# Carrying a running phase between token groups by a one-row transfer instead of running sums and half of the carry products

## The chip, the cores and the metric

The kernel runs on one core of a Trainium2 chip. The metric is device time in microseconds (us); results below are medians of executions. Each execution also has a mean granted TensorE clock (1.0 is full speed). With a single core, "slow" only labels an execution over 1.5% above the fastest of the same kernel in the same call.

A word on names: PE is TensorE, DVE VectorE, ACT ScalarE, POOL GpSimd. "L302" is line 302 of that kernel's source; the changed kernel is 12 lines shorter, so the same line has a smaller number there.

## The reference

The work is a gated linear attention with complex decay, followed by a gated mixture feed-forward block. What matters here is the phase.

```python
batch, n_heads, seq, head_dim = (4, 8, 768, 48)
a_re_n, a_im_n = (a_re * scale, a_im * scale)      # scale limits |a| to 0.999
for t in range(S):
    new_re = ar * S_re - ai * S_im                 # state times a complex number
    new_im = ar * S_im + ai * S_re
    S_re, S_im = (new_re + k_t v_t^T, new_im)
    y[t] = q_t . S_re
# ... then, on x = y of 3072 tokens x 384:
g = x @ w_gate                                     # 384 x 1536
ffn_out = (gelu(g) * (x @ w_val)) @ w_out
out = x + sigmoid(x @ w_res) * ffn_out
```

(Condensed.) A product of complex numbers over tokens is a product of magnitudes and a sum of angles. So the kernel needs, for every head and channel (8 x 48 = 384 columns), the running sum of angles over 768 tokens of a batch.

## The kernel before

The 3072 tokens are cut into 12 groups of 256 tokens: four batches times three groups (s = 0, 1, 2), the batches taken in turn. A group lies on 128 partitions in two halves (c = 0, 1). Groups are worked in units: [0], [1,2], [3,4] ... [11]. While one unit is in its attention and output phase, the angles of the next unit are summed. A sum over tokens is a sum over partitions, so it is a TensorE product with a triangular matrix. What earlier groups and halves leave behind comes in as a second product, with a matrix of equal elements (`ones2pi`), over a tile that holds the running sum of the batch's earlier angle tiles (from the second half of its first group on).

```python
    def carry(g):
        b, s = ORD[g]
        if s > 0:
            P = T["R", b]
            nc.vector.tensor_tensor(out=P, in0=P, in1=T["th", g][:, 0:DM], op=OP.add)      # L279
            T["P", g] = P

    def carry_on(g):
        b, s = ORD[g]
        if s == 0:
            T["R", b] = st1.tile([128, DM], FP, tag="R%d" % b, name="R")
            nc.vector.tensor_copy(out=T["R", b], in_=T["th", g][:, DM:W])                  # L287
        elif s < NS - 1:
            nc.vector.tensor_tensor(out=T["R", b], in0=T["R", b], in1=T["th", g][:, DM:W], op=OP.add)   # L289

    def cs_t(g, c):
        # ... (tiles named, cut)
        cs = psM.tile([128, DM], FP, tag="mm", padded_shape=[128, 512], name="cst")
        nc.tensor.matmul(out=cs, lhsT=tmat[c], rhs=th[:, sl], start=True, stop=(s == 0))   # L300
        if s > 0:
            nc.tensor.matmul(out=cs, lhsT=ones2pi, rhs=T["P", g], start=False, stop=True)  # L302
        f = T["f", g]                                                                      # phase in turns,
        nc.vector.tensor_scalar(out=f[:, sl], in0=cs, scalar1=MAGIC, scalar2=MAGIC, op0=OP.add, op1=OP.subtract)
        nc.vector.tensor_tensor(out=f[:, sl], in0=cs, in1=f[:, sl], op=OP.subtract)        # less whole turns
        if c == C - 1:
            carry_on(g)
            # ... (absolute value for the cosine, cut)
```

`tmat[1]` is a triangular matrix that sums the tokens up to each token; `tmat[0]` is the same matrix less its constant. The trick lies in the difference: with P holding half 0 of this group, the product with `ones2pi` adds the whole of half 0, which the negative triangle of `tmat[0]` then corrects. One tile P so serves both halves.

The place of these steps in the program is set by a list of steps that is woven with the others by fractions of the stage:

```python
        cst = [f for g in g1 for f in [call(carry, g)] + [call(cs_t, g, c) for c in range(C)]]
        # ...
            weave((0.0, 0.05, pn[:2]), (0.06, 0.1, csls), (0.12, 0.25, pn[2:]), (0.26, 0.4, exs),
                  # ... (cut)
                  (0.5, 0.5, dec), (0.55, 0.65, atn), (0.62, 0.8, cst), (0.9, 0.95, sin), ...)
            return
        # ...
        weave((0.0, 0.12, csls), ..., (0.46, 0.46, dec), (0.2, 0.65, cst), (0.7, 0.95, atn + sin), ...)
```

Of the kernel before, what the change touches and what calls it, by code (L numbers as in the profile page):

```python
# [9 lines left out]
FP = mybir.dt.float32  # L10
BF = mybir.dt.bfloat16
AF = mybir.ActivationFunctionType
OP = mybir.AluOpType
# [3 lines left out]
def weave(*streams):  # L17

    order = []
    for si, (begin, end, steps) in enumerate(streams):  # L20
        n = len(steps)
        for i, step in enumerate(steps):
            order.append((begin + (end - begin) * (i + 0.5) / n, si, i, step))
    for _, _, _, step in sorted(order, key=lambda e: e[:3]):
        step()
# [3 lines left out]
def kernel(  # L29
# [13 lines left out]
    nc = tc.nc  # L43
    B, H, S, D = q.shape
    DD = 2 * D
    DM = H * D
# [3 lines left out]
    C = 2  # L50
    W = C * DM
    NS = S // (128 * C)
# [3 lines left out]
    ORD = [(b, s) for s in range(NS) for b in range(B)]  # L56
# [19 lines left out]
    tmat = []  # L76
# [9 lines left out]
    ones2pi = singles.tile([128, 128], FP, name="ones2pi")  # L86
# [28 lines left out]
    st1 = ctx.enter_context(tc.tile_pool(name="st1", bufs=1))  # L115
# [13 lines left out]
    T = {}  # L129
# [78 lines left out]
    def squares(g):  # L208

        def q0():  # L210
            T["lm", g] = pS.tile([128, W], FP, tag="s", name="lm")
            with paced("gelu"):
                nc.scalar.activation(out=T["lm", g], in_=flat(T["ar", g]), func=AF.Square)

        def q1():
            if g < 5:
                if g == 0:
                    T["sq"] = hb.tile([128, 4, 2, DM], FP, tag="h2", name="sq0")
                t = T["sq"][:, g % 4].rearrange("p a m -> p (a m)")
            else:  # L220
                t = pE.tile([128, W], FP, tag="E", name="sq")
            T["sq", g] = t
            if g in DVSQ:
                nc.vector.tensor_tensor(out=t, in0=flat(T["ai", g]), in1=flat(T["ai", g]), op=OP.mult)
            else:
                with paced("gelu"):
                    nc.scalar.activation(out=t, in_=flat(T["ai", g]), func=AF.Square)  # L227

        def q2():
            with paced("gmul"):  # L230
                nc.vector.tensor_tensor(out=T["lm", g], in0=T["lm", g], in1=T["sq", g], op=OP.add)  # L231
        return [q0, q1, q2]

    def p1_steps(g):

        def s0():
            lm = T["lm", g]
            act(out=lm, in_=lm, func=AF.Ln)
            nc.vector.tensor_scalar(out=lm, in0=lm, scalar1=0.5, scalar2=LNMAX, op0=OP.mult, op1=OP.min)  # L239

        def s1():
            ar = flat(T["ar", g])
            T["s", g] = pE.tile([128, W], FP, tag="E" if g == 1 else "Ei", name="ra") if g in (1, 2) else ar
            act(out=T["s", g], in_=ar, func=AF.Ln)

        def s2():
            T["th", g] = flat(T["ai", g])
            act(out=T["s", g], in_=T["s", g], func=AF.Exp, scale=-1.0)
            nc.vector.tensor_tensor(out=T["th", g], in0=T["s", g], in1=T["th", g], op=OP.mult)
        return [s0, s1, s2]  # L250
# [5 lines left out]
    def cs_l(g, c):  # L256
        if c == 0:
            if g == 0:
                t = hb.tile([128, 4, DM], FP, tag="sg", name="E0")
                T["E", g] = t[:, 0:2].rearrange("p a m -> p (a m)")  # L260
                T["Ei", g] = t[:, 2:4].rearrange("p a m -> p (a m)")
            else:
                T["E", g] = pE.tile([128, W], FP, tag="E", name="E")
                T["Ei", g] = pE.tile([128, W], FP, tag="Ei", name="Ei")
        sl = slice(c * DM, (c + 1) * DM)
        cs = psM.tile([128, DM], FP, tag="mm", padded_shape=[128, 512], name="csl")
        nc.tensor.matmul(out=cs, lhsT=lmat[c], rhs=T["lm", g][:, sl], start=True, stop=True)  # L267

        def ex():
            act(out=T["E", g][:, sl], in_=cs, func=AF.Exp)  # L270
            act(out=T["Ei", g][:, sl], in_=cs, func=AF.Exp, scale=-1.0)
        return ex

    def carry(g):

        b, s = ORD[g]
        if s > 0:
            P = T["R", b]
            nc.vector.tensor_tensor(out=P, in0=P, in1=T["th", g][:, 0:DM], op=OP.add)  # L279
            T["P", g] = P  # L280

    def carry_on(g):

        b, s = ORD[g]
        if s == 0:
            T["R", b] = st1.tile([128, DM], FP, tag="R%d" % b, name="R")
            nc.vector.tensor_copy(out=T["R", b], in_=T["th", g][:, DM:W])  # L287
        elif s < NS - 1:
            nc.vector.tensor_tensor(out=T["R", b], in0=T["R", b], in1=T["th", g][:, DM:W], op=OP.add)  # L289

    def cs_t(g, c):
        s = ORD[g][1]
        th = T["th", g]
        if c == 0:
            if ("f", g) not in T:
                T["f", g] = T["lm", g]
            T["af", g] = th
        sl = slice(c * DM, (c + 1) * DM)
        cs = psM.tile([128, DM], FP, tag="mm", padded_shape=[128, 512], name="cst")
        nc.tensor.matmul(out=cs, lhsT=tmat[c], rhs=th[:, sl], start=True, stop=(s == 0))  # L300
        if s > 0:
            nc.tensor.matmul(out=cs, lhsT=ones2pi, rhs=T["P", g], start=False, stop=True)  # L302
        f = T["f", g]
        nc.vector.tensor_scalar(out=f[:, sl], in0=cs, scalar1=MAGIC, scalar2=MAGIC, op0=OP.add, op1=OP.subtract)
        nc.vector.tensor_tensor(out=f[:, sl], in0=cs, in1=f[:, sl], op=OP.subtract)
        if c == C - 1:
            carry_on(g)
            T["abs"] = nc.vector.tensor_scalar(out=T["af", g].bitcast(mybir.dt.int32), in0=f.bitcast(mybir.dt.int32),
                                    scalar1=0x7FFFFFFF, scalar2=None, op0=OP.bitwise_and)

# [317 lines left out]
    def gs(u):  # L628
        return UNITS[u] if 0 <= u < NU else []
# [7 lines left out]
    def call(f, *a):  # L637
        return lambda: f(*a)
# [4 lines left out]
    def att_steps(u, half):  # L643

        todo = [(g, c, i * C + c) for i, g in enumerate(gs(u)) for c in range(C)]
        n = len(todo) // 2
        steps = []
        for i, (g, c, jj) in enumerate(todo[half * n:half * n + n]):
            steps += attention(g, c)
            if i > 0:  # L650
                steps.insert(-1, call(xt_step, u, jj - 1))
        if n:
            steps.append(call(xt_step, u, half * n + n - 1))
        return steps

    def phase_x(u):

        pend = []
        g1 = gs(u + 1)
        p1g = [g for w in range(NU) if P1AT.get(w, w - 2) == u for g in gs(w)]  # L660
        now = [g for g in p1g if g in g1]
        ahead = [g for g in p1g if g not in g1]
        ops = [call(op_step, u - 1, jj) for jj in range(len(gs(u - 1)) * C)]
        att = att_steps(u, 1)
        if not g1:
            weave((0.0, 0.8, att), (0.1, 1.0, ops))
            return

        def csl(g, c):
            pend.append(cs_l(g, c))  # L670

        def ex():
            pend.pop(0)()

        def p1(g):
            return (squares(g) if g == HELD else []) + p1_steps(g) + [call(decay0, g)]
        csls = [call(csl, g, c) for g in g1 for c in range(C)]
        exs = [ex for _ in g1 for _ in range(C)]
        dec = [call(decay2, g) for g in g1]
        cst = [f for g in g1 for f in [call(carry, g)] + [call(cs_t, g, c) for c in range(C)]]  # L680
        sin = [call(p2_sin, g) for g in g1]
        table("natural_log_exp_and_others")()
        if now:
            atn = [table("trig_and_small")] + [call(p1_arctan, g) for g in now + ahead]
            pn = zip_steps([p1(g) for g in now])
            weave((0.0, 0.05, pn[:2]), (0.06, 0.1, csls), (0.12, 0.25, pn[2:]), (0.26, 0.4, exs),
                  (0.28, 0.48, zip_steps([p1(g) for g in ahead])),
                  (0.5, 0.5, dec), (0.55, 0.65, atn), (0.62, 0.8, cst), (0.9, 0.95, sin),
                  (0.0, 0.8, att), (0.0, 0.25, ops) if u == 1 else (0.1, 1.0, ops))
            return  # L690
        atn = [table("trig_and_small")] + [call(p1_arctan, g) for g in ahead]
        weave((0.0, 0.12, csls), (0.05, 0.5, zip_steps([p1(g) for g in ahead])), (0.12, 0.45, exs),
              (0.46, 0.46, dec), (0.2, 0.65, cst), (0.7, 0.95, atn + sin), (0.0, 0.8, att), (0.1, 1.0, ops))
# [141 lines left out]
```

## Time and profile before

The median was 298.79 us (298.38 to 299.6) over three executions. The profiled execution has a span of 297.3 us.

From 119 us on, the kernel is a string of alternating stages, and three and a half of them hold the angle sums. The windows view of the kernel before (columns: from and to, length, then busy us and records of each engine, clock, DMA share, GB/s) gives the part up to the first output product of unit 1, then the three full stretches (from the first output product to the first gate product of the next stage) and the last one, which has one group:

```profile
0.00:119.24 119.24, 81.50 (x603) 50.91 (x607) 90.09 (x160) 87.99 (x143) 35.63 (x59) 0.87 1.28 176
119.24:134.93 15.69, 15.11 (x111) 9.42 (x110) 15.14 (x28) 13.76 (x23) 9.10 (x14) 1.00 0.99 142
159.77:175.45 15.68, 15.11 (x111) 9.42 (x111) 15.29 (x27) 13.76 (x23) 9.36 (x13) 1.00 1.01 129
200.65:216.09 15.44, 14.87 (x112) 9.33 (x111) 14.45 (x25) 10.23 (x18) 10.78 (x14) 1.00 0.70 74
238.23:252.36 14.13, 12.68 (x110) 7.97 (x109) 10.54 (x17) 7.19 (x11) 4.71 (x6) 1.00 0.49 82
```

In the three full stretches TensorE is busy 96% of the time, but VectorE about as much: 15.14 us of 15.69 in the first. That is what makes the change hard to price. The instructions that it touches, from the records of their source lines (duration as least/median/most in ns, first and last start in us, form):

```profile
L302 PE MATMUL cst<-R,ones2pi x32: 486/486/486, 84.7 to 245.8; 128*128 128x384 f32 x32
...
L279 DVE TENSOR_TENSOR R<-R,ai x8: 545/550/550, 51.5 to 209.3; 128x384 f32<-128x384 f32 x8
...
L289 DVE TENSOR_TENSOR R<-R,ai x4: 544/546/547, 89.7 to 166.4; 128x384 f32<-128x384 f32 x4
```

There are 16 carry products, recorded as 32 (an fp32 product shows as two). The last view is the chain of waits of the kernel before, as start, length and what it was. It shows what a carry product costs in the chain, 0.65 us and not twice 0.486, and it shows the long wait of the first part:

```profile
54.70 11.83 DMA ai<-in_a_im_dram
...
121.55 0.73 PE cst L300 x2
122.29 0.65 PE cst L302 x2
```

### The profile page before, as it was taken

To read this page: it belongs to the slowest core of one execution; us is meant where nothing else is said; L and a number is where in the kernel's file an instruction comes from. 1 tells how busy PE (TensorE), PEld (TensorE's weight loads), DVE (VectorE), ACT (ScalarE), POOL (GpSimd) and SP (SyncE) were. 2 spreads that over 40 slices of the span, in tenths; PEclk is the share of its full clock that TensorE was granted. 3 is DMA by queue.
4 is the path that set the end of the run, shared out by engine and by line. 5 is a ranking of instruction groups with operands and counts; after the bars stand their busy time and mean duration, and the time that the engine had idled before them with its cause. 6 is when DMAs were issued, how large, how long until landed. Compare 5 with 4: busy or idle time off the path is not lost.

```text
span 297.3 us, 5158 instructions
## 1 busy us (share of the span) xinstructions
PE 250.2 (84%) x1850; PEld 150.7 (51%) x1864; DVE 226.5 (76%) x404; ACT 196.1 (66%) x325; POOL 91.3 (31%) x133
## 2 busy tenths in 40 slices
PE   0345866848895999999999999989999998999994
PEld 0122445736552456554556654556545664455782
DVE  0789986864799777999897997879967776574452
ACT  3876899736989388975679964677564655445250
POOL 4020941400444204374305381224911232010220
PEclk9968775986999899999999999999999999999999
DMA  9999999999996999959999989999499646810631
GB/s 148 187 174 188 174 198 188 170 179 195 175 166 130 158 211 175 169 114 182 216 169 167 111 127 187 192 165 70 66 212 210 101 48 124 176 29 0 160 57 53
DMA packets 175746, 44.00 MB, mean 148 GB/s; under 512 B 164836, under 2 KB 175720, under 8 KB 175720
## 3 DMA queue, kind: packets, MB, share of 16 engines
q1 hardware_dynamic: 140744, 33.05, 64.4%
q0 software_dynamic: 34976, 10.63, 34.2%
q8 instruction: 14, 0.23, 0.3%
q14 instruction: 12, 0.10, 0.1%
HBM read 31.33 MB, written 9.08 MB: 136 GB/s over the span
## 4 chain that ended last, share of the span: by engine, by line
PE 63%; ACT 15%; DVE 10%; DMA 5%; issue 4%; SPq 1%; DVEq 0%; ACTq 0%
PE vp L591 14%; PE gp L587 14%; PE op L611 14%; DMA ai<-in_a_im_dram 5%; PE cst L300 5%; ACT L625 3%; PE cst L302 3%; PE rp L603 3%; PE csl L267 2%; PE at L438 2%; ACT ar L140 2%; PE tpx L572 1%; PE dk L480 1%; ACT CS L140 1%; SPq L160 1%
## 5 line engine op out<-in xcount | busy, mean ns | idle before, releaser
L140 ACT ACTIVATE h<-gp 128x512 bf16<-128x512 f32 (+1 forms) x84 | 44.8, 536 | 45.0 <-PE gp L587 44.6
L594 DVE SCALAR_TENSOR_TENSOR h<-h,vp 128x512 bf16<-128x512 bf16 (+1 forms) x84 | 50.6, 607 | 25.6 <-PE vp L591 17.8
L587 PE MATMUL gp<-xT,wg 128*128 128x512 bf16 (+1 forms) x238 | 62.4, 358 | 4.0 <-ACT h L140 1.8
L591 PE MATMUL vp<-xT,wv 128*128 128x512 bf16 (+1 forms) x252 | 63.1, 358 | 0.0
L611 PE MATMUL op<-wo,h 128*128 128x384 bf16 x288 | 50.7, 326 | 1.1 <-ACT Ei L140 0.7
L620 POOL DMA_DIRECT2D out_dram<-x x22 | 20.5, 951 | 57.5 <-DMA out_dram<-ot 53.9
L591 PEld LDWEIGHTS <-wv 128*128 128x128 bf16 x252 | 25.2, 101 | 23.0 <-issue 1.2
L611 PEld LDWEIGHTS <-h 128*128 128x128 bf16 x288 | 27.3, 98 | 17.9 <-issue 2.0
L587 PEld LDWEIGHTS <-wg 128*128 128x128 bf16 x252 | 24.3, 101 | 21.6 <-issue 5.0
L323 POOL DMA_DIRECT2D m<-d x32 | 24.1, 775 | 28.0 <-DMA d<-Ei 17.0
L174 POOL DMA_DIRECT2D v<-in_v_dram x24 | 21.9, 920 | 29.5 <-DMA ai<-in_a_im_dram 23.9
L625 ACT ACT_TABLE_LOAD x21 | 26.9, 1283 | 1.1 <-PEq L819 0.7
L441 DVE TENSOR_TENSOR atm<-at,mask 128x512 bf16<-128x512 f32 x36 | 24.5, 681 | 2.3 <-PE at L438 2.3
L197 POOL COPY landed<-k 1x1 f32<-1x1 f32 x9 | 2.8, 310 | 66.0 <-DMA k<-in_k_dram 66.0
L267 PE MATMUL csl<-lm,lt0a 128*128 128x384 f32 x24 | 11.7, 574 | 10.9 <-DVE lm L239 10.9
L614 DVE SCALAR_TENSOR_TENSOR ot<-sg,op 128x384 f32<-128x384 f32 x24 | 13.2, 548 | 9.9 <-PE op L611 8.6
L493 ACT CAST x<-y 128x384 bf16<-128x384 f32 x22 | 10.6, 480 | 12.9 <-PE y L490 12.8
L300 PE MATMUL cst<-ai,lt0b 128*128 128x384 f32 x24 | 11.8, 578 | 6.4 <-ACT ai L140 6.0
L231 DVE TENSOR_TENSOR lm<-lm,sq 128x768 f32<-128x768 f32 x12 | 11.4, 950 | 7.1 <-ACT sq L227 6.9
L140 ACT ACTIVATE ar<-ar 128x768 f32<-128x768 f32 x20 | 16.8, 853 | 0.0
L572 PE MATMUL tpx<-ident,x 128*128 128x128 bf16 x72 | 8.3, 230 | 9.5 <-ACT h L140 4.8
L140 ACT ACTIVATE sg<-rp 128x384 f32<-128x384 f32 x24 | 11.6, 490 | 6.2 <-PE rp L603 6.2
(112 smaller groups left out, 486.7 us busy)
## 6 DMA issues: line engine op xcount, KB each, us to landing
ar<-in_a_re_dram SPq DMA_DIRECT2D x24, 192.0 KB, 5.5
ai<-in_a_im_dram SPq DMA_DIRECT2D x24, 192.0 KB, 4.7
q<-in_q_dram SPq DMA_DIRECT2D x24, 192.0 KB, 4.8
k<-in_k_dram SPq DMA_DIRECT2D x24, 192.0 KB, 4.9
out_dram<-ot SPq DMA_DIRECT2D x24, 192.0 KB, 2.6
out_dram<-x POOLq DMA_DIRECT2D x22, 192.0 KB, 4.5
v<-in_v_dram POOLq DMA_DIRECT2D x24, 96.0 KB, 5.3
wg<-in_moe_w_gate_dram POOLq DMA_DIRECT2D x4, 288.0 KB, 7.9
```

The lines of the kernel that those rows point to most:

```text
L140: return tab(nc.scalar.activation(**kw))
L174: held(nc.gpsimd.dma_start(out=t[:, c], in_=rows(v, g, c)), after)
L267: nc.tensor.matmul(out=cs, lhsT=lmat[c], rhs=T["lm", g][:, sl], start=True, stop=True)
L300: nc.tensor.matmul(out=cs, lhsT=tmat[c], rhs=th[:, sl], start=True, stop=(s == 0))
L323: nc.gpsimd.dma_start(out=m[u * D:(u + 1) * D].rearrange("p r h -> p (r h)"), in_=md.rearrange("r (h d) -> d (r h)", h=H))
L441: nc.vector.tensor_tensor(out=atm, in0=at, in1=mask4, op=OP.mult)
L587: nc.tensor.matmul(out=gp, lhsT=wg[:, fi, ffi * 128:(ffi + 1) * 128], rhs=xT[:, fi, :], start=(fi == 0), stop=(fi == KD - 1))
L591: nc.tensor.matmul(out=vp, lhsT=wv[:, fi, ffi * 128:(ffi + 1) * 128], rhs=xT[:, fi, :], start=(fi == 0), stop=(fi == KD - 1))
L594: T["gmul"] = nc.vector.scalar_tensor_tensor(out=h2[:, ffi, :], in0=h2[:, ffi, :], scalar=0.5, in1=vp, op0=OP.mult, op1=OP.mult)
L611: nc.tensor.matmul(out=ps, lhsT=h2[:, ffi, jj * 128:(jj + 1) * 128], rhs=wo[:, ffi, :], start=(ffi == 0), stop=(ffi == KF - 1))
L620: nc.gpsimd.dma_start(out=out[t0:t0 + 128, :], in_=T["x", token(u, jj)], accum_op=OP.add)
L625: tab(nc.scalar.preload_act_table_set(nm))
```

## The change

The idea is to need no running sum. The phase of the previous group's last token, already reduced to a fraction of a turn, holds all that went before (whole turns do not matter). It is row 127 of the second half of f. That row, 384 numbers or 1.5 KB, is moved by a transfer from partition 127 to partition 0, and added, times 2 pi, to the first token's angle of the batch's next group. Then half 0 needs only the triangle; half 1 needs the triangle and one product over half 0.

```diff
-    def carry(g):
-        b, s = ORD[g]
-        if s > 0:
-            P = T["R", b]
-            nc.vector.tensor_tensor(out=P, in0=P, in1=T["th", g][:, 0:DM], op=OP.add)
-            T["P", g] = P
-
-    def carry_on(g):
-        (a copy for s == 0, an add for s == 1; cut)
     def cs_t(g, c):
+        if s > 0 and c == 0:
+            nc.vector.scalar_tensor_tensor(out=th[0:1, sl], in0=T["row", b], scalar=2.0 * math.pi, in1=th[0:1, sl],
+                                           op0=OP.mult, op1=OP.add)
-        nc.tensor.matmul(out=cs, lhsT=tmat[c], rhs=th[:, sl], start=True, stop=(s == 0))
-        if s > 0:
-            nc.tensor.matmul(out=cs, lhsT=ones2pi, rhs=T["P", g], start=False, stop=True)
+        nc.tensor.matmul(out=cs, lhsT=tmat[c if s == 0 else 1], rhs=th[:, sl], start=True, stop=(s == 0 or c == 0))
+        if s > 0 and c > 0:
+            nc.tensor.matmul(out=cs, lhsT=ones2pi, rhs=th[:, 0:DM], start=False, stop=True)
         (...)
         if c == C - 1:
-            carry_on(g)
+            if s < NS - 1:
+                T["row", b] = st1.tile([1, DM], FP, tag="R%d" % b, name="row")
+                nc.gpsimd.dma_start(out=T["row", b], in_=f[127:128, sl])
-        cst = [f for g in g1 for f in [call(carry, g)] + [call(cs_t, g, c) for c in range(C)]]
+        cst = [call(cs_t, g, c) for g in g1 for c in range(C)]
```

It removes 8 of 16 carry products, four copies and four adds of 128x384; eight adds shrink to one partition; eight small transfers are new. The woven list also falls from six steps to four for a unit, so the remaining steps land at other places among the steps around them.

More of the change, by code (lines that the diff above doesn't have):

```diff
@@ L272, in cs_l, with cs_t @@
         return ex
-    def carry(g):
+    def cs_t(g, c):
         b, s = ORD[g]
-        if s > 0:
-            P = T["R", b]
-            nc.vector.tensor_tensor(out=P, in0=P, in1=T["th", g][:, 0:DM], op=OP.add)
-            T["P", g] = P
-    def carry_on(g):
-        b, s = ORD[g]
-        if s == 0:
-            T["R", b] = st1.tile([128, DM], FP, tag="R%d" % b, name="R")
-            nc.vector.tensor_copy(out=T["R", b], in_=T["th", g][:, DM:W])
-        elif s < NS - 1:
-            nc.vector.tensor_tensor(out=T["R", b], in0=T["R", b], in1=T["th", g][:, DM:W], op=OP.add)
-    def cs_t(g, c):
-        s = ORD[g][1]
         th = T["th", g]
```

## The prediction

> **What bounds the kernel now.** Over the span TensorE is 84% busy, VectorE 76%, ScalarE 66% (busy shares); the chain that ended last is 63% TensorE. By stage (the windows view): from 119.2 to 135.7 us TensorE is busy 15.82 of 16.5 us, VectorE 15.95; from 159.8 to 176.2 TensorE 15.78, VectorE 16.02 of 16.4; from 198.2 to 216.9 TensorE 18.08 of 18.7. These are the three full stretches in which a unit's angles are summed between the output matmuls, at full granted clock; the chain runs through the angle matmuls (L300, L302) there. The ramp (to about 75 us) is bound by transfers (the chain waits 11.83 us for a load of a_im, to 66.5 us), by VectorE, and by a throttled clock (0.72 to 0.83). From 80 to 96 us VectorE (15.82 of 16.0 us) and ScalarE bind.
>
> **What the change removes.** Eight groups have a carry. Before, each of their two halves added a carry product; now only the second half adds the first half's sums. So 8 of 16 fp32 carry products go (16 of 32 recorded matmuls). A recorded one lasts 486 ns, but they overlap: in the chain two take 0.65 us. 8 x 0.65 = 5.2 us of TensorE.
>
> VectorE loses 4 copies (0.36 us each) and 4 running-sum adds (0.55): 3.6 us. The 8 adds of L279 (0.55) become adds on one partition with the same 384 elements. [...] I cost them at 0.55 too.
>
> **What it adds.** Eight 1.5 KB transfers on GpSimd's queue. Like ones (d<-E, d<-Ei) take 0.5 us of issue and land after 3.5 to 4.4 us. A row is used tens of us later, so landing is off the critical path. Order could hurt: [...] the compiled order puts three rows before the second group's v and all weight loads. But those wait for loads until 29.82 and 31.93 us anyway, and the three phase rows are finished at 24.6, about 27 and 29.6 us: at most 0.5 us of delay.
>
> **How much is on the critical path.** The three full stretches carry two groups each: 3 x 2 x 0.65 = 3.9 us; VectorE, nearly as full there, loses 1.1 and 0.55 us in the first two, so it should follow, perhaps not wholly. The last stretch (238 to 252 us, one group) 0.65. The 80 to 96 us stretch loses one copy and one add on VectorE: about 0.5. Ramp: near 0, plus or minus 0.5, because transfers set its end. The tail from 271 us is unchanged. Sum 4.5 to 5; the compiled order of VectorE and TensorE is also reshuffled, worth plus or minus 1.
>
> **Predicted: 294.3 us**, 8 in 10 between 292.4 and 297.5. Faster by over 2% (below 292.8): 0.14; within 2%: 0.84; slower: 0.02.
>
> **What would show it.** Carry records fall from 32 to 16, TensorE busy by about 5 us, VectorE by about 3.6; the one-partition adds last about 0.55 us and wait for no transfer; each full stretch, from first output matmul to first gate matmul, is about 1.3 us shorter with TensorE still over 95% busy; weight loads issue within 0.5 us of 31.9; the a_im landing at 66.5 us moves by under 0.5 us.
>
> **What would make it wrong.** VectorE or ScalarE ending the full stretches, so that TensorE idles for what it saved; the reordered GpSimd queue delaying weights, v or result adds by microseconds; the reshuffled ramp delaying the a_im load, on which everything after it waits; or an unforeseen gain, if the ramp's copies sat on its chain.

The price of the one-partition adds is the author's estimate, from the 0.55 us that the adds on 128 partitions took. The forecast's sum, 3.9 us for the full stretches, 0.65 for the last and about 0.5 for the 80 to 96 us stretch, with the ramp at 0 plus or minus 0.5, was put at 4.5 to 5 us, and 298.8 less 4.5 is the 294.3 us. The adds count in it as neither gain nor loss.

## More of the kernel before

The page of the kernel before: first the busy time of each engine with its share of the span, then the granted TensorE clock in 40 slices of 7.4 us (a digit is tenths of full speed; 9 is 90% or more), then the engines' shares of the chain that ended last.

```profile
PE 250.2 (84%) x1850; PEld 150.7 (51%) x1864; DVE 226.5 (76%) x404; ACT 196.1 (66%) x325; POOL 91.3 (31%) x133
...
PEclk9968775986999899999999999999999999999999
...
PE 63%; ACT 15%; DVE 10%; DMA 5%; issue 4%; SPq 1%; DVEq 0%; ACTq 0%
```

TensorE has the largest share, but the clock line already shows two regimes. Up to about 105 us the clock dips again and again; after that it is full.

## The result, and the profile after

| | executions | median us | range us |
|---|---|---|---|
| before | 4 | 298.75 | 298.38 to 299.60 |
| after | 4 | 297.12 | 296.87 to 297.44 |

The ratio is 0.9942, 95% interval 0.9918 to 0.9966. A ratio here is the mean time of one kernel's fast runs over that of the other's of the same rounds, so it is not quite the ratio of the medians. The result lies inside the predicted range and in the predicted class, but the gain is 1.63 us where 4.5 were forecast: about a third.

The page after, the same lines:

```profile
PE 249.4 (84%) x1848; PEld 149.8 (51%) x1848; DVE 224.1 (76%) x396; ACT 197.1 (67%) x325; POOL 95.5 (32%) x141
...
PEclk9968675797999599999999999999999999999998
...
PE 57%; DMA 15%; ACT 12%; DVE 8%; issue 4%; POOL 2%; SPq 1%; DVEq 0%; ACTq 0%
```

TensorE fell by only 0.8 us of busy time. (The number of records falls by 2 where 16 carry records went, because the trace before lacks 14 of its 252 gate products, L587; so its busy time is somewhat understated.) The clock line has changed: the thirteenth and fourteenth slices, 89 to 103 us, were 9 and 8 and are now 9 and 5. The windows after, cut at the same landmarks:

```profile
0.00:121.73 121.73, 84.40 (x605) 52.52 (x605) 89.24 (x155) 88.65 (x143) 39.76 (x64) 0.85 1.29 174
121.73:136.14 14.41, 13.83 (x106) 8.75 (x106) 13.96 (x25) 13.67 (x23) 8.62 (x14) 1.00 1.00 141
160.99:175.39 14.40, 13.83 (x106) 8.75 (x106) 13.86 (x25) 13.66 (x23) 7.78 (x12) 1.00 1.02 135
201.09:215.24 14.15, 13.58 (x108) 8.54 (x107) 13.76 (x24) 9.58 (x17) 8.18 (x12) 1.00 0.69 66
237.59:250.53 12.94, 11.99 (x109) 7.60 (x108) 10.10 (x17) 7.21 (x11) 4.87 (x7) 1.00 0.68 94
```

The four stretches are shorter by 1.28, 1.28, 1.29 and 1.19 us, 5.04 us in all, which is more than the 4.5 forecast. And the first window is longer by 2.49 us: the first output product of unit 1 starts at 121.73 instead of 119.24. In it TensorE is busy 2.90 us longer for nearly the same matmuls (605 against 603 records; the trace before lacks 3 gate products here) at a lower clock (0.85 against 0.87). The changed instructions themselves, from their lines' records after:

```profile
L288 PE MATMUL cst<-ai,ones2pi x16: 486/486/486, 86.0 to 244.2; 128*128 128x384 f32 x16
...
L283 DVE SCALAR_TENSOR_TENSOR ai<-row,ai x8: 536/539/541, 52.5 to 215.2; 1x384 f32<-1x384 f32 x8
...
DMA to landing us min/median/max: 2.6/4.1/5.0
```

The carry records are halved, the add on one partition takes 539 ns where the add on 128 took 550, and a row lands 2.6 to 5.0 us (median 4.1) after its issue, tens of us before its use.

The DMA share of the chain rose from 5% to 15%. Part of that is in the ramp, where the chain after runs through the third row's issue (29.96 us, in GpSimd's timeline of call 2), the v and weight issues behind it, and two loads, to the first gate product (start, length and what it was):

```profile
30.45 1.93 POOL v L174 x2
34.61 7.95 DMA wv<-in_moe_w_val_dram
42.84 5.22 DMA v<-in_v_dram
48.07 0.80 PE gp L575 x3
```

That product started at 46.80 us before. But in a second trace of the kernel before, without rows, it started at 48.09, so the path alone does not show that the rows cost time; call 2 below tests it.

For an account of the time I read the same landmarks from the timelines of both kernels (start of the square that waits for the a_im load; the three ScalarE table loads A, B, C after it; the first output product of each unit; the first gate product of each later stage). The table is worked out, not a view. "Plain repeats" are later traces of the same two files: one of the kernel before and three of the changed one (one of these in an execution labelled slow, 297.3 us, beside a lucky 292.62).

| stage | before | after | difference | in plain repeats |
|---|---|---|---|---|
| start to the a_im square | 66.62 | 67.17 | +0.55 | before 65.00; after 67.29 to 67.81 |
| square to table load A | 7.57 | 7.61 | +0.04 | before 6.12; after 7.54 to 8.56 |
| A to B | 13.88 | 14.48 | +0.60 | before 14.16; after 14.48 each time |
| B to C | 6.01 | 6.01 | 0 | the same |
| C to first output product | 25.16 | 26.47 | +1.31 | before 23.70; after 25.30 to 26.44 |
| four stretches | 60.94 | 55.90 | -5.04 | before 60.94; after 55.91 to 56.04 |
| stages between them and the tail | 117.15 | 117.84 | +0.69 | before 117.15; after 117.43 to 118.62 |

The differences sum to -1.85 us, the difference of the spans (297.33 and 295.48 unrounded). So the gain did not go missing where it was earned. It was given back before 122 us, and a little of it in the later gate stages.

### The half-speed windows

The granted clock is not a smooth quantity in these traces. Apart from the edges it is either full (1.00) or half (0.50), and the half-speed stretches are multiples of 3.41 us: the clock records of the kernel before have half speed at 17.1 to 23.9, 30.7 to 34.2, 41.0 to 51.2, 64.9 to 71.7 and 95.6 to 99.0 us, all of 3.4, 6.8 or 10.2 us. Within a trace the stretches start whole steps of 3.41 us apart (17.09 and 95.60 us are 23 steps apart; so are 17.49 and 96.00 in the changed kernel); one such step is called a window here. From trace to trace the steps lie differently: 0.4 us later in the changed kernel's first trace than in that of the kernel before, and 2.1 us later in `k_order` (half speed from 97.73 us).

The last of these is where the 1.31 us went. TensorE's timeline before, where the second gate stage resumes after a wait (start, length of the group, instruction, and in brackets the idle time before it and what ended it):

```profile
94.41 0.54 PE L480 MATMUL dk<-v,padK 128*96 128x48 bf16 x8 [1.05 <-DVE padK L373]
96.02 1.44 PE L587 MATMUL gp<-xT,wg 128*128 128x512 bf16 x3 [1.07 <-ACT h L140]
97.25 1.49 PE L591 MATMUL vp<-xT,wv 128*128 128x512 bf16 x3
98.53 1.06 PE L587 MATMUL gp<-xT,wg 128*128 128x512 bf16 x3
99.42 0.81 PE L591 MATMUL vp<-xT,wv 128*128 128x512 bf16 x3
```

And after:

```profile
95.60 0.54 PE L468 MATMUL dk<-v,padK 128*96 128x48 bf16 x8 [2.93 <-DVE padK L361]
97.20 1.44 PE L575 MATMUL gp<-xT,wg 128*128 128x512 bf16 x3 [1.07 <-ACT h L140]
...
101.00 1.48 PE L579 MATMUL vp<-xT,wv 128*128 128x512 bf16 x3
102.28 1.09 PE L575 MATMUL gp<-xT,wg 128*128 128x512 bf16 x3
103.20 0.81 PE L579 MATMUL vp<-xT,wv 128*128 128x512 bf16 x3
```

Before, the dense run starts at 96.02, 0.4 us into a half-speed window (95.6 to 99.0), and full speed returns at its end. After, it starts at 97.20, 1.2 us into one (96.0 to 99.4); full speed returns only at the end of the next, at 102.8. From group start to group start, three products take 1.28 us at half speed and 0.65 at full. So a start that lay 0.8 us deeper in its window went with a whole further window at half speed; the other 0.4 us of the 1.2 us delay is how much later the windows themselves lay.

The other traces show the same. Eleven of those without idle products have half speed here. In the three in which the dense run starts 1.20 to 1.27 us into a window (the changed kernel twice, and `c_rows_late`), the half speed lasts two windows; in the eight in which it starts at most 0.72 us into one, or up to 0.53 us before one, it lasts one. (In `d_warm` of call 1 it starts 1.26 us into one, but idle products already run from 97.8 us, 0.8 us before that window; the half speed lasts one.) And the stage goes by that number. In the fourteen traces with no idle products, or only the first and too small set of them, it takes from table load C to the first output product 23.70 or 23.71 us with no half-speed window (two traces), 25.10 to 25.63 with one (nine), 26.44 to 26.48 with two (three), over both kernels and their variants.

The two fences show one more difference: ahead of the eight `dk` products TensorE is idle for 1.05 us before and 2.93 us after. Before, another 1.01 us of idleness comes earlier (at 90.61 us), with two steps of gate products between the two; after, those steps run first and the waits have joined. All eight traces of the changed kernel and its variants without idle products have 2.87 to 2.94 us in one piece here, and one or two half-speed windows; the four of the kernel before, with or without rows alone, have the two shorter pieces, and none or one. So the new order, and not only the later start, may bring half speed. No run tests the two apart.

It would be too simple to say that the change always adds this one window. Two of the three repeats of the changed kernel had only one here (25.30 and 25.32), but then had 6.8 or 10.2 us of half speed around table load A, where that stage took 8.53 or 8.56 us instead of 7.61. The sum hardly moves: the first output product of unit 1 starts at 121.61 to 122.18 us in all four traces of the changed kernel, against 119.24 and 114.99 in the two of the kernel before.

### The order on VectorE

The 0.60 us between table loads A and B is something else. VectorE's timeline before, up to the angle product that comes ahead of table load B:

```profile
79.68 0.56 DVE L304 TENSOR_SCALAR lm<-cst 128x384 f32<-128x384 f32 x1
80.15 0.68 DVE L464 TENSOR_TENSOR atm<-at,mask 128x512 bf16<-128x512 f32 x1
80.75 0.95 DVE L249 TENSOR_TENSOR ai<-ar,ai 128x768 f32<-128x768 f32 x1
```

And after:

```profile
79.88 0.56 DVE L290 TENSOR_SCALAR lm<-cst 128x384 f32<-128x384 f32 x1 [0.61 <-PE cst L286]
80.36 0.41 DVE L445 COPY qk<-tp 96x512 bf16<-96x512 bf16 x1
80.69 0.54 DVE L291 TENSOR_TENSOR lm<-cst,lm 128x384 f32<-128x384 f32 x1
81.26 0.69 DVE L452 TENSOR_TENSOR atm<-at,mask 128x512 bf16<-128x512 f32 x1
81.87 0.95 DVE L249 TENSOR_TENSOR ai<-ar,ai 128x768 f32<-128x768 f32 x1
```

The subtraction of an angle half (L291 after, L305 before) has moved ahead of the product L249 on this full engine, by 0.54 us. A copy (L445) has moved ahead of it too. Here the weave puts the shortened list elsewhere. The product starts 1.12 us later; 0.59 of that was already there at table load A.

### The profile page after: what moved, and what is told of

It is laid out like the page before. It is cut to its first block, busy times and chain, and to the rows that moved or that the text cites. A ratio compares the mean times of both kernels' runs of the same rounds, so it can differ in the third digit from the quotient of the medians.

```text
span 295.5 us, 5144 instructions
## 1 busy us (share of the span) xinstructions
PE 249.4 (84%) x1848; PEld 149.8 (51%) x1848; DVE 224.1 (76%) x396; ACT 197.1 (67%) x325; POOL 95.5 (32%) x141
## 4 chain that ended last, share of the span: by engine, by line
PE 57%; DMA 15%; ACT 12%; DVE 8%; issue 4%; POOL 2%; SPq 1%; DVEq 0%; ACTq 0%
PE op L599 14%; PE vp L579 13%; PE gp L575 13%; DMA ai<-in_a_im_dram 6%; PE cst L286 5%; DMA KT<-padK 3%; DMA wv<-in_moe_w_val_dram 3%; ACT L613 3%; PE rp L591 3%; PE at L426 2%; DMA v<-in_v_dram 2%; DMA ar<-in_a_re_dram 2%; PE cst L288 2%; PE dk L468 1%; PE csl L267 1%
## 5 line engine op out<-in xcount | busy, mean ns | idle before, releaser
L575 PE MATMUL gp<-xT,wg 128*128 128x512 bf16 (+1 forms) x252 | 64.5, 365 | 1.5 <-ACT h L140 1.1
L579 PE MATMUL vp<-xT,wv 128*128 128x512 bf16 (+1 forms) x252 | 64.1, 363 | 0.0
L311 POOL DMA_DIRECT2D m<-d x32 | 23.9, 776 | 27.8 <-DMA d<-Ei 15.4
L174 POOL DMA_DIRECT2D v<-in_v_dram x24 | 22.9, 958 | 17.9 <-DMA ai<-in_a_im_dram 11.8
L267 PE MATMUL csl<-lm,lt0a 128*128 128x384 f32 x24 | 12.5, 607 | 11.1 <-DVE lm L239 11.1
L286 PE MATMUL cst<-ai,ut0b 128*128 128x384 f32 x40 | 17.8, 533 | 0.3 <-ACT Ei L140 0.3
L140 ACT ACTIVATE CS<-ai,hpi 128x768 bf16<-128x768 f32 x12 | 11.2, 932 | 6.4 <-DVE ai L296 6.4
```

The costliest lines, as they stand in the source:

```text
L140: return tab(nc.scalar.activation(**kw))
L174: held(nc.gpsimd.dma_start(out=t[:, c], in_=rows(v, g, c)), after)
L267: nc.tensor.matmul(out=cs, lhsT=lmat[c], rhs=T["lm", g][:, sl], start=True, stop=True)
L286: nc.tensor.matmul(out=cs, lhsT=tmat[c if s == 0 else 1], rhs=th[:, sl], start=True, stop=(s == 0 or c == 0))
L311: nc.gpsimd.dma_start(out=m[u * D:(u + 1) * D].rearrange("p r h -> p (r h)"), in_=md.rearrange("r (h d) -> d (r h)", h=H))
L575: nc.tensor.matmul(out=gp, lhsT=wg[:, fi, ffi * 128:(ffi + 1) * 128], rhs=xT[:, fi, :], start=(fi == 0), stop=(fi == KD - 1))
```

## The experiments

Three theories were set against each other.

- The clock theory (theory 1 where a recorded text counts them and says nothing else): the savings in the stretches are real, and they are given back because TensorE starts its early dense stages a little later and meets more half-speed windows.
- The queue theory (theory 2): the eight row transfers, on GpSimd's queue, delay v and the weights, and so the start.
- The full-engine rival: VectorE or ScalarE binds in the stretches, so removing TensorE's work there gains less than its cost.

Together they are 18 runs. All gave the reference's result within tolerance. "Idle products" below are TensorE products into scratch PSUM that nobody reads. The runs of one call shared a chip and the executions of the kernel before.

### Call 1: is the saving real, and does simple warming help?

`a_repeat` is the changed kernel again. `b_putback` puts back eight carry products of the same size, ahead of the triangle of half 0; the triangle starts the sum anew, so the result stays right.

```diff
+        if s > 0 and c == 0:
+            nc.tensor.matmul(out=cs, lhsT=ones2pi, rhs=th[:, sl], start=True, stop=True)
         nc.tensor.matmul(out=cs, lhsT=tmat[c if s == 0 else 1], rhs=th[:, sl], start=True, stop=(s == 0 or c == 0))
```

`d_warm` is the changed kernel with 17 idle products, `e_before_warm` the kernel before with the same ones. That such products in TensorE's waits keep the clock up was the assumption; calls 1, 4 and 5 show what they did:

```diff
+    def warm(pool, tag, rhs, n):
+        t = pool.tile([128, 512], FP, tag=tag, name="warm")
+        for _ in range(n):
+            nc.tensor.matmul(out=t, lhsT=ident, rhs=rhs, start=True, stop=True)
@@ ramp: after the first group's sines
+        warm(psD, "dk", T["CS", g0].rearrange("p x u d -> p (x u d)")[:, 0:512], 8)
@@ after group 3's K is padded: 5;  second step of the gate stage of unit 1: 4
+                    warm(psT, "tp", pads[nm, g % 2][:, 0:4].rearrange("p x d -> p (x d)"), 5)
+            warm(psT, "tp", xT[:, 0, :], 4)
```

> The changed kernel again, for a second trace. Theory 1 (clock): the change saved 5.0 us of TensorE on the critical path (1.28, 1.28, 1.29 in the three full stretches, 1.19 in the last), and lost 1.27 us in the ramp and 1.31 us in the second gate stage because two granted-clock windows of 3.41 us stayed at half speed there; then the landmarks of this trace move with the position of the half-speed windows, by about 1.3 us for each window more or less, while the four stretches repeat to 0.1 us. Theory 2 (GpSimd order): the ramp loses the same 1.0 to 1.3 us before the first gate product whatever the clock did. Either: 296.9 to 297.4 us.

> The changed kernel with the eight removed fp32 products put back as work only (a product of the same size whose result the next one overwrites; result unchanged). Theory 1 (the 5 us were saved in full and something else gave 3 us back): 5.0 us slower than the changed kernel, about 302 us, slower than before. Rival (VectorE or ScalarE bind the full stretches, so only about 1.6 us of the 5 was ever to be had): 298.5 to 299 us, like before.

> The changed kernel with 17 idle products that nobody reads, in TensorE's waits: 8 in the ramp ahead of the first transposes, 9 ahead of the second gate stage[...]. Theory 1: no half-speed window at 96 us and one fewer at 31 us, the second gate stage shorter by about 1.7 to 3 us; total 294 to 295.5 us. Theory 2 (GpSimd order, or VectorE reshuffling): within 0.4 us of the changed kernel.

> The kernel before with the same idle products. Theory 1: it too loses its half-speed windows at 31 and 96 us, 1 to 2.5 us, to about 297; the pair of kernels with idle products then differs by about 4.5 to 5 us, the amount that was predicted. Theory 2: 298.7 us, and the pair differs by 1.6 us.

| run | median us | range us | mean us |
|---|---|---|---|
| before, 7 executions | 300.04 | 294.38 to 301.90 | 298.98 |
| a_repeat | 297.73 | 294.06 to 299.17 | 297.17 |
| b_putback | 301.14 | 300.62 to 301.59 | 301.12 |
| d_warm | 297.31 | 296.85 to 298.06 | 297.38 |
| e_before_warm | 297.93 | 294.59 to 299.56 | 297.51 |

The first surprise is the kernel before: on this chip it ranged over 7.5 us. The four executions of the first comparison, within 1.2 us, had hidden that. The fast-only ratio of `a_repeat`, 1.0003 (0.985 to 1.016), compares with the three fastest of seven and says little.

`b_putback` took back the whole gain: ratio to before 1.0159 (1.0072 to 1.0246), and 3.4 us by medians above `a_repeat`. (The ratio uses only the fast three of the kernel before; against the median of all seven it is 1.1 us slower.) Its windows for the first and the last stretch:

```profile
122.16:137.76 15.60, 15.02 (x110) 9.48 (x110) 15.26 (x26) 13.70 (x23) 8.11 (x13) 1.00 0.94 142
...
240.98:254.57 13.59, 12.63 (x110) 7.98 (x109) 10.10 (x17) 7.20 (x11) 4.29 (x6) 1.00 0.36 75
```

The full stretches are back to 15.60, 15.59 and 15.44 us (before 15.69, 15.68, 15.44), although nothing came back on VectorE's list. So TensorE binds there, and the full-engine rival falls: 4.31 of the 5.04 us in the four stretches came back. In the last stretch the one group's product returned 0.65 us, as priced; the other 0.54 of its 1.19 us came with the change and not with the product. The first output product was at 122.16 us, as in `a_repeat` (122.18): the loss of the first part does not come back with the products either (one trace each).

The warming missed its expectation. `d_warm` still had half speed at 64.4 to 74.6 and 98.5 to 101.9 us; the idle products did not fill the wait for a_im at 60 to 67 us. The pair `e_before_warm` and `d_warm` differs by 0.6 us by medians and 0.1 by means, where the clock theory expected 4.5 to 5 and the queue theory 1.6. Since the clock was not held up in `d_warm`, the pair does not test the clock theory, but it gives it no support either.

### Call 2: the row transfers

`c_rows_late` issues the three rows of the ramp only after the last weight load (the orders of TensorE, VectorE and ScalarE stay identical). `j_rows_alone` is the kernel before plus eight row transfers alone, into device memory that nobody reads (again with identical orders on the three engines).

```diff
 c_rows_late
-                nc.gpsimd.dma_start(out=T["row", b], in_=f[127:128, sl])
+                with tc.issue_after(T["ld", "w", 3].ins) if g < 3 else nullcontext():
+                    nc.gpsimd.dma_start(out=T["row", b], in_=f[127:128, sl])
 j_rows_alone, on the kernel before
+            if s < NS - 1:
+                nc.gpsimd.dma_start(out=dr.tile([1, DM], FP, tag="rw", name="rw"), in_=f[127:128, sl])
```

> The kernel before, for a second trace of it on this chip. All theories: second weight group issued by GpSimd at 31.9 us, a_im load of the wait at 66 to 67 us, the four stretches last 15.69, 15.68, 15.44 and 14.13 us as in the first trace; what moves between runs is the part before 119 us. A spread of several us in it with the same program would say that one trace pair cannot price the ramp.

> The changed kernel. Theory 2 (GpSimd order): the second half of the second group's v is issued 0.8 to 1.9 us later than before, the first weight load 0.5 to 1.5 us later, and the first output matmul of the second gate stage's unit (119.24 us before) 1.5 to 3 us later. The stretches 14.41, 14.40, 14.15 and 12.94 us as in two traces.

> The changed kernel with the ramp's three row transfers held behind the last weight load in GpSimd's order; the orders of TensorE, VectorE and ScalarE are unchanged. Theory 2: v and weights are issued as before the change (weights at 31.9 us), the loads that follow land 0.5 to 1.4 us earlier than in the changed kernel, and the total falls by 0.5 to 1.5 us (to about 296 where the changed kernel takes 297). Theory 1 (clock windows alone): issue times move, the total does not.

> The kernel before plus the eight row transfers alone, from the same rows at the same places of GpSimd's order, into memory that nobody reads; the orders of TensorE, VectorE and ScalarE are those of before. Theory 2: slower than before by 0.5 to 1.5 us, all of it lost before the first output matmul at 119 us, weights issued at 32.4 to 33.4 us. Theory 1: same as before within 0.3 us apart from the clock windows.

GpSimd's timeline of the kernel before, at the first weight load:

```profile
29.82 1.75 POOL L174 DMA_DIRECT2D v<-in_v_dram  x2 [12.15 <-DMA ai<-in_a_im_dram]
31.93 0.75 POOL L181 DMA_DIRECT2D wg<-in_moe_w_gate_dram  x1 [0.36 <-DMA q<-in_q_dram]
```

And after:

```profile
29.96 0.48 POOL L295 DMA_DIRECT2D row<-ar  x1 [1.99 <-DVE ar L291]
30.44 1.94 POOL L174 DMA_DIRECT2D v<-in_v_dram  x2
32.36 0.77 POOL L181 DMA_DIRECT2D wg<-in_moe_w_gate_dram  x1
```

The delay is there: 0.43 us in this trace, 1.47 in `a_repeat` (33.40), where the issue of the v pair took 2.89 us instead of 1.75. `c_rows_late` took it away (first weight load at 31.93 again), and the time stayed: 296.83 us (296.09 to 297.66) against 296.9 (292.62 to 297.30) of `after_again`. `j_rows_alone` was at 300.59 (296.82 to 301.32) against 299.01 (295.34 to 300.52) before; the interval of its ratio, 1.0052 (0.9938 to 1.0166), holds one, but its mean is 1.5 us above. `after_again` had the delays that the queue theory expected (first weight load at 32.57 us); whether they cost time, only `c_rows_late` and `j_rows_alone` can tell. `before_again` was at 297.92 (294.89 to 301.29).

The traces of this call show the spread of the kernel before itself. `before_again` was profiled in a lucky execution, 294.89 us: no half-speed window after 59 us, 23.70 us for the C stage, first output product at 114.99 us instead of 119.24. From there to the end it took 178.1 us, as the first trace did (297.33 - 119.24 = 178.09). All of the difference between the two is in the first part.

### Call 3: order, and the rows again

`k_order` moves the angle steps of the first woven stage later, to undo the order change on VectorE; `n_order_late` is that with the rows late; `j2_rows_alone` and `l_after` repeat with more executions.

```diff
-               (0.46, 0.46, dec), (0.2, 0.65, cst), (0.7, 0.95, atn + sin), ...
+               (0.46, 0.46, dec), (*((0.3, 0.65) if u == 1 else (0.2, 0.65)), cst), (0.7, 0.95, atn + sin), ...
```

> The changed kernel, as the reference of this call. From the second gate stage's end on it repeats to 0.1 us; before that it spreads by some us. Mean 1.5 to 2.5 us below before.

> The changed kernel with the angle steps of the first unit-pair stretch alone emitted later (between 0.3 and 0.65 of that phase in place of 0.2 and 0.65), so that two angle operations fewer, 0.47 us net by the durations in the traces, stand on VectorE ahead of the angle product that the second table load waits for. If the lost 0.60 us between the first and the second table load (14.48 us in every trace with the change, 13.88 in three of four without it) comes from VectorE's order: 13.9 to 14.1 us in the trace, and the total about 0.5 us less than the changed kernel's. If it comes from the row transfers on GpSimd: 14.48 again.

> Both mendings: that order, and the ramp's row transfers behind the weights. If both losses are real and add: 1.0 to 2.0 us below the changed kernel, about 295 where it takes 297, with weights issued at 31.9 us. If the transfers' place does not matter for the total: the same as k_order within 0.3 us.

> The kernel before plus the row transfers alone, a second time with more rounds, because its first result (1.6 us slower by medians) has an interval that holds zero. If GpSimd's order costs what the first showed: 1.0 to 2.0 us slower than before. If that was the spread of the ramp: within 0.5 us of before.

| run | median us | range us | ratio to before (95%) |
|---|---|---|---|
| before, 11 executions | 299.49 | 296.54 to 301.17 | |
| l_after | 298.13 | 296.56 to 298.52 | 0.9952 (0.9898 to 1.0005) |
| k_order | 296.17 | 294.07 to 299.26 | 0.9889 (0.9833 to 0.9946) |
| n_order_late | 296.33 | 295.65 to 297.68 | 0.9913 (0.9865 to 0.9961) |
| j2_rows_alone | 300.08 | 299.39 to 301.70 | 1.0042 (0.9992 to 1.0091) |

`k_order` recovered only 0.15 us between A and B (14.33; 13.9 to 14.1 was expected), so the edit did not do what it was meant for. Its total is lower than `l_after`'s by 1.3 us by means (296.36 and 297.71), but the ranges overlap, and the stage it aimed at does not explain that. Rows late on top made no difference (0.16 us). `j2_rows_alone` is 0.6 us slower than the kernel before by medians and 1.3 by means, between its two expectations; the interval just holds one. The order theory for the 0.60 us is therefore seen in the timelines and not confirmed by an undoing. (In call 4 the same edit went with 13.60 us in `s_best_warm2` against 14.23 in `q_after_warm2`, but there the stage before it was 1.8 us longer, so that settles nothing.)

### Call 4: holding the clock up in both kernels

Now idle products fill every long TensorE wait up to 98 us, the a_im wait among them, in both kernels alike. The edit is the same in `p_before_warm2` (kernel before) and `q_after_warm2` (changed kernel); `r_rows_warm2` is p plus the eight rows alone; `s_best_warm2` is q with rows late and the order of `k_order`.

```diff
+    def warm(pool, tag, rhs, n, lhsT=None):
+        t = pool.tile([128, 512], FP, tag=tag, name="warm")
+        for _ in range(n):
+            nc.tensor.matmul(out=t[:, 0:rhs.shape[1]], lhsT=ident if lhsT is None else lhsT, rhs=rhs, start=True, stop=True)
+        warm(psD, "dk", T["CS", g0].rearrange("p x u d -> p (x u d)")[:, 0:512], 8)     # ramp
+        ..., lambda: warm(psT, "tp", T["x", 0], 8), ...                                  # at about 45 us
+            if g == 5:
+                warm(psT, "tp", T["lm", g][:, 0:512], 7, lmat[1])                        # fp32, in the a_im wait
+                    warm(psT, "tp", pads[nm, g % 2][:, 0:4].rearrange("p x d -> p (x d)"), 5)
+            warm(psT, "tp", xT[:, 0, :], 12)                                             # ahead of the second gate stage
```

> The kernel before with idle products in the long waits of TensorE up to 98 us (30 of bf16 and 7 of fp32 that nobody reads). If the clock makes the spread: no or one half-speed window between 60 and 105 us, executions within about 2 us of each other, mean 295 to 297 us.

> The changed kernel with the same idle products; the compiled orders of the two then nearly agree before 119 us. If the clock took most of what was given back: 3.5 to 5 us below the kernel before with idle products. If the row transfers did: 2.5 to 3.5 us below. If neither: 1.5 to 2 us below, as without idle products.

> The kernel before with idle products plus the row transfers alone. If GpSimd's order costs what the two calls without idle products suggest: 1.0 to 1.5 us slower than the kernel before with idle products. If their cost went through the clock, or was spread: within 0.5 us of it.

> The changed kernel with idle products, the ramp's rows behind the weights and the later angle steps in the first stretch. If the two losses are real: 0.5 to 1.5 us below the changed kernel with idle products, 291 to 294 us, faster than both kernels by 1% or more.

| run, 6 executions each | median us | range us | ratio to before (95%) |
|---|---|---|---|
| before, 11 executions | 299.17 | 296.93 to 300.87 | |
| p_before_warm2 | 298.80 | 297.93 to 302.10 | 1.0012 (0.9945 to 1.0078) |
| q_after_warm2 | 293.67 | 293.18 to 295.26 | 0.9822 (0.9771 to 0.9872) |
| r_rows_warm2 | 298.77 | 298.21 to 299.54 | 0.9986 (0.9936 to 1.0036) |
| s_best_warm2 | 296.69 | 295.45 to 297.45 | 0.9917 (0.9863 to 0.9971) |

With the clock held up after 60 us, q is 5.1 us below p by medians, 5.7 by means (299.61 and 293.92), instead of 1.6. The clock lines of p and of q:

```profile
PEclk9969977999999999999999999999999999999999
```

```profile
PEclk9999968799999999999999999999999999999999
```

Neither has a dip after the eighth slice (60 us). In the traces the first output product of unit 1 is at 118.09 us in p and 118.49 in q: the change costs 0.40 us there, not 2.49. But 1.1 us of the gap between p and q is not the change's: the C stage took 25.00 us in p and r without any half-speed window in it, 23.92 in q and s, because the same idle products came at a less good place among p's instructions. Less that, the change is worth about 4 us here, and the loss at the first output product would be about 1.5 us. The kernel before missed its expectation (a mean of 295 to 297 us, a spread of about 2): p is no faster than without idle products and spreads over 4.2 us, and only its fastest execution has a trace. So the clock after 60 us is not all that makes executions differ.

`r_rows_warm2` against p is -0.03 us by medians, within intervals of 0.5%. `c_rows_late` and `n_order_late` removed the delay from the changed kernel and gained nothing. So no run shows that the rows' place in GpSimd's queue costs the changed kernel anything. But without idle products the rows alone made the kernel before 1.5 and 1.3 us slower by means, with intervals that just hold one, so that a cost of the rows of about a microsecond is not excluded.

`s_best_warm2` was meant to be the best and was 3 us slower than q. Its trace had half speed at 52.3 to 59.2 us (q at 52.5 to 56.0); TensorE was 2.2 us late by then, the block of fp32 idle products ran from 63.07 instead of 60.83, and so overshot the a_im wait: the stage from square to A took 9.27 us instead of 7.46. So these idle products ran on to 70.4 us although the wait that they were meant to fill was over at 67.3, when the square started.

### Call 5: a shorter dose, placed alike

`v_before_warm3` and `x_after_warm3` repeat the comparison with five fp32 idle products instead of seven, none after K is padded, and 14 instead of 12 ahead of the second gate stage.

```diff
-                warm(psT, "tp", T["lm", g][:, 0:512], 7, lmat[1])
+                warm(psT, "tp", T["lm", g][:, 0:512], 5, lmat[1])
-                    warm(psT, "tp", pads[nm, g % 2][:, 0:4].rearrange("p x d -> p (x d)"), 5)
-            warm(psT, "tp", xT[:, 0, :], 12)
+            warm(psT, "tp", xT[:, 0, :], 14)
```

> The kernel before with the trimmed idle products: no half-speed window between 60 and 105 us, second gate stage from table load to first output matmul 23.7 to 24.2 us. Mean 296 to 298.5 us.

> The changed kernel with the same. If what the change gave back went through the clock: 3.5 to 4.8 us below the kernel before with trimmed idle products, 292.5 to 294.5 us, and faster than both kernels of the comparison. If the 1.1 us of placement and luck made the first pair's difference: 1.5 to 3 us below.

The kernel before was at 297.98 us in this call (294.52 to 301.36, eleven executions), v at 297.71 (296.39 to 299.15), x at 294.76 (292.87 to 295.94). The change is worth 2.95 us by medians, 3.2 by means (297.77 and 294.55): by medians still at the top of what was expected without the clock (1.5 to 3), by means between that and the clock theory's 3.5 to 4.8. In the traces the first output product is at 118.14 us in v and 118.59 in x (+0.45), the C stage 23.92 and 23.71, and the spans are 296.23 and 292.29, -3.94 us, which is inside the clock theory's range: four stretches -4.98, the first part +0.45, the later gate stages +0.60. (The trace of x still has one half-speed window, at 70.4 to 73.8 us; that of v has none after 59.1.)

### What the plain executions say together

Over all calls there are 55 executions of the plain kernel before, mean 298.65 and median 299.01 us (294.38 to 301.90), and 18 of the changed one, mean 297.07 and median 297.28 (292.62 to 299.17). The difference of the means, 1.6 us, is the first result again, over several chips. Of the kernel before, 6 of 55 were below 295.5 us; of the changed one 2 of 18.

## Why the prediction was right or wrong

Right:

- What binds the full stretches. TensorE does: 13.83 of 14.41 us after, 96%. Each got shorter by 1.28 or 1.29 us, as forecast to 0.02, in every plain trace within 0.2, and put-back products gave most of it back (the full stretches to within 0.1 us).
- The one-partition add at 0.55 us: 0.539 measured. The price was an estimate from the add on 128 partitions, and the trace agrees: 1x384 takes 539 ns, 128x384 took 550.
- Rows landing off the critical path (2.6 to 5.0 us; no add waited for one), the weights delayed by under 0.5 us in the first trace (0.43; but 1.47 in `a_repeat`), and the tail unchanged (25.69 and 25.67 us from the last unit but one's outputs to the end).

Mis-sized, without weight in the total:

- The last stretch gave 1.19 us and not 0.65. The product was worth 0.65, as the put-back shows; 0.54 came with the rest of the change.
- "TensorE busy by about 5 us" was 0.8. In the four stretches TensorE's busy time did fall by 4.54 us (1.28, 1.28, 1.29, 0.69); in the first part it rose by 2.90 at the lower clock; the rest is the records that the trace before lacks in its gate stages. Busy time was not work here: 605 matmul records took 84.40 us at a clock of 0.85 where 603 took 81.50 at 0.87. VectorE fell by 2.4 us and not 3.6.

Wrong, and this decided the outcome, was the step "Ramp: near 0, plus or minus 0.5, because transfers set its end", and with it "the 80 to 96 us stretch ... about 0.5" of gain. It took the early part as fixed by transfers and by a clock that the change doesn't touch. Measured in the first pair of traces, the first output product of unit 1 came 2.49 us later where about 0.5 us earlier had been forecast. The terms are:

- One more half-speed window of 3.41 us in the second gate stage: +1.31 us in this pair. Shown: without idle products the C stage takes 23.7, 25.1 to 25.6 or 26.45 us by the number of such windows, which goes with where in a window the dense run starts (two when 1.20 to 1.27 us into one, one when at most 0.72; `d_warm` apart). With the clock held up in both kernels the loss at the first output product is 0.45 us (call 5) instead of 2.49; the 0.40 of call 4 is flattered by 1.1 us of placement. It was partly chance that this pair showed it: two of the three repeats had no second window here.
- +0.60 us between table loads A and B, where 0.5 had been forecast as a gain. It is 14.48 in all plain traces of the changed kernel, and the order on VectorE differs there. But the one edit that aimed at it recovered 0.15, the kernel before has 14.16 in its second trace, and with idle products the stage takes 14.16 in the kernel before (p, v) and 14.23 in the changed one (q, x). So the order is a reading of the timelines and not a proven cost.
- +0.55 us until the a_im square, which the forecast held to under 0.5. One pair of traces can't price it, but all twenty agree on the direction: the square starts at 64.9 to 66.6 us in the five of the kernel before without rows, and at 66.75 to 68.9 in the fifteen that have the change or row transfers alone (means of 65.8 us for the five and 67.5 for the twelve with the change). Holding the ramp's rows back did not bring it forward (67.0 to 67.5). Why it is later is open.

Smaller losses followed in the later gate stages, +0.69 us in the first pair. The chain after has a wait of 8.41 us for a transposed K that the chain before has not. Whether the changed order or chance brings it is open.

The forecast also listed "the reshuffled ramp delaying the a_im load, on which everything after it waits" and "the reordered GpSimd queue" as dangers. The first is what the late square looks like. The second was real as a delay, and taking it away gained nothing. That clock windows set part of the loss was not on the list, although the profile before showed a clock of 0.75 from 17 to 45 us and 0.78 from 45 to 75.

So the failed step is the ramp and the 80 to 96 us stretch, taken as fixed and as a small gain; what the runs showed in its place is a first part that came 2.49 us later, 1.31 of it by a further half-speed window, the rest with the late square and the stage from A to B, whose causes are not shown.

What stays open is the exact share of the clock. The gain rose from 1.6 us to 3.0 (call 5) and 5.1 (call 4, of which about 1.1 is placement), so if the whole rise is the clock's, its share is between 1.4 and 2.4 us of what was missing (2.9 against the forecast, 3.4 against the 5.04 of the stretches). Single executions of either kernel spread by 6 to 7 us, and the number of half-speed windows was read only where there was a trace. The six executions each of v and x put the difference of their means, 3.2 us, at 1.8 to 4.7 (an estimate of the 95% interval from their spread), so the rise over 1.6 is barely clear of the noise.

The best version is the changed kernel with idle products, `q_after_warm2`: 293.67 us, 0.9822 times the kernel before in its call, 5.5 us below by medians. The idle products alone gained nothing in the kernel before (p and v: ratios 1.0012 and 1.0045, both intervals hold one).

## What to carry to other kernels

Price a removal stage by stage, between landmarks that both traces have: here every saturated stretch gave what the instruction cost in the chain (0.65 us a product), and most of the loss lay in a part that the removed work hardly touches. In this kernel's early part, which alternates waits and dense TensorE work, a start 1.2 instead of 0.4 us into a half-speed window went with a whole further one and 1.31 us more, so look at several executions' clocks before calling such a part fixed, look at whether the new order joins short waits into a long one, and put the spread of the ramp into the forecast. With idle products the clock stayed up here after 60 us (no half-speed window in the traces of p, q and v, one in x), but they need waits of dependable length: in `s_best_warm2` the fixed dose began 2.2 us late and overshot (9.27 us from square to A instead of 7.46).
